# Causal attention and a PReLU MLP on one core: sums of x ahead of ACT's rounding, one w_out decode later, w_in pieces three slots sooner

## Chip, core and metric

The kernel runs on one core of a Trainium2 chip. The metric is the device time of one execution in microseconds (us), as the median of several runs. The core's engines work beside each other, each through a queue of its own in program order: PE (TensorE: matrix products into PSUM), DVE (VectorE), ACT (ScalarE), POOL (GpSimd), and SP (SyncE), which here issues nearly all transfers between HBM and SBUF.

## What is computed

```python
def _attn_ref(q, k, v):
    scores = scale * np.matmul(q, k.transpose(0, 1, 3, 2))
    scores = np.where(mask, -1000000000.0, scores)
    scores = scores - np.max(scores, axis=-1, keepdims=True)
    attn = np.exp(scores)
    attn = attn / (np.sum(attn, axis=-1, keepdims=True) + 1e-09)
    return np.matmul(attn, v).astype(np.float32)

def _moe_ref(x, w_in, w_out, alpha):
    h = x @ w_in
    g = np.maximum(h, 0.0) + alpha * np.minimum(h, 0.0)
    return (g @ w_out).astype(np.float32)
```

There are 4 batches of 12 heads, 448 positions, 64 dimensions a head. The attention's output, laid out as 1792 tokens of 768 features, is x; w_in is 768 by 2048, w_out 2048 by 768. Both weights arrive as 64-bit floats and are turned into 32-bit ones on the core.

## The kernel before

**Two stages.** The attention handles 24 pairs of heads; the MLP follows and takes about two thirds of the time. The MLP's products are done in a rounded 32-bit format, so each operand is split in a high part (rounded by ACT, a copy with a change of type) and a low part (the operand minus its high part, on DVE or POOL), and three products stand for one. The first product also saves multiplications by working with sums and differences of blocks of x and w_in: T1 to T4 are sums over x, S1 to S4 over w_in.

**The attention's order** is written out by hand in the string `ORDER`. `attention` (a loop over rounds n) goes through its words; `XF+4` means "step XF for pair n - 4". A step issues its instructions on its engine at that place of the program, so the string fixes the order within each queue. In one round PE does the product with v (AV), the 448-wide scores (S2), the transposes (PT1, PT0, PT2, PT3) and the scores of the next pair (S0, S1). DVE does the row maxima (MX), the two transpose copies C00 and C21 and the reciprocal (RC). ACT does the exponentials (EX) and the other transpose copies (C10, C20, C30). POOL normalises (NO). For x, when AV of a pair is done, four steps read its result from one PSUM bank: XH rounds it on ACT (blocks "B"), XN rounds it on DVE (blocks "N"), XF forms the sums on DVE (one or two operations per pair, line 545, and for some pairs a copy), XL takes the low part on DVE (line 553), after which the bank is free. PSUM has eight banks, handed out in turn.

**Weights between the attention's steps.** A piece of weights is loaded by SP into one of two raw buffers (`load_next`), then: `abs` on ACT (line 243), `clamp` on POOL (246), four operations "D" on DVE (249, 253, 256, 257), the last of which frees the raw buffer, and `add` on POOL (260). A finished piece is rounded by `cast` on ACT and its low part taken by `sub` on POOL (291 for w_in, 320 for w_out). The tables `EARLY` and `FRONT` give, for each round, what of this is done: i0 to i3 are the four w_in pieces of a group g, o0 to o3 those of w_out. In them A is abs, C clamp, D:i:k are k operations of piece i, + is add, LD a load, T the high and low part of one of the sums T on POOL. `FRONT` is done at the round's start (step E2), `EARLY` at step ED, between the low part and the copies C00 and C21; casts and abs of rounds before 24 at the step EA, behind the last transposes and C30.

**Behind the attention.** Round 26 also holds products of the first MLP group (`h_plain`, hooks behind AV and C30) and the PReLU of h (`h_act`, lines 721 and 722, on DVE). Then a table `FIRST` gives slots 0 to 30. In each of slots 1 to 10 PE does one `h_plain`, in each of slots 11 to 30 one `o_half` (a 128 by 384 part of the second product, line 769, put into SBUF by ACT at line 775). Around it the slot's tasks are issued: first act, gh and gl (PReLU; high part of g on ACT, line 731; low part on POOL, line 735), then D, then the rest in the order of `KINDS`. `.1` stands for pieces of the second group (g = 1). th and tl are high and low part of a T (ACT line 394, DVE line 569), st stores them, S forms a sum of w_in on DVE (265). Slot 23's `o_half` is the first that needs g_X of the second column block (gh.1X, gl.1X). After slot 30 the groups g = 1 to 7 follow in a fixed cycle.

Of the kernel before, what the change touches and what calls it, by code (L numbers as in the profile page):

```python
# [24 lines left out]
EARLY = {  # L25
# [5 lines left out]
}  # L31
FRONT = {25: "D:4:4", 26: "+:5 A:6 A:7"}
LOADV = {0: 2, 1: 2, 2: 2, 3: 1, 9: 4, 10: 3, 12: 1, 13: 2, 14: 2, 15: 2}
TURNS = [(0, 0), (0, 1), (0, 2), (0, 5), (1, 0), (1, 1), (1, 3), (1, 4), (0, 3), (0, 4), (1, 2), (1, 5)]
ORDER = """
E2+4 LK+0 LQ+0 LT+4 NO00+3p NO10+3p MX11+2 NO21+3p NO11+3p EX10+2 EX11+2 MX20+2 NO20+3p MX21+2 EX20+2 NO30+3p MX00+2 EX00+2 AV+4 S2+2 LV+4 PT1+3 PT0+3 PT2+3 XH+4 EX21+2 MX01+2 EX01+2 C10+3a XN+4 MX30+2 XF+4 XL+4 EX30+2 ED+4 C00+3d C21+3d RC+2 NO01+2p C20+3a PT3+3 S0+1 S1+1 SF+1 C30+3a EA+4 MX10+1 ST+4
"""
FIRST = """
0: gh.0Y gh.0X gl.0Y gl.0X cast.o0.0 cast.o1.0
1: act.0Z gh.0W gl.0W sub.o0.0 sub.o1.0 cast.o2.0 cast.o3.0  # L40
2: gh.0Z gl.0Z sub.o2.0 abs.i0.1 th
3: sub.o3.0 clamp.i0.1 tl th
4: D.i0.1.2 abs.i1.1 tl
5: act.1Y act.1X D.i0.1.2 load clamp.i1.1
6: gh.1Y D.i1.1.2 add.i0.1
7: gl.1Y D.i1.1.2 load th
8: add.i1.1 tl th
9: tl
10: S.S1.1 th abs.i2.1
11: act.1W act.1Z clamp.i2.1 cast.S1.1  # L50
12: D.i2.1.2 sub.S1.1 tl
13: D.i2.1.2 load th cast.L1.1
14: add.i2.1 abs.i3.1 tl th sub.L1.1
15: clamp.i3.1 S.S2.1 tl cast.A22.1
16: D.i3.1.2 cast.A11.1 sub.A22.1 st
17: gh.1X D.i3.1.2 load cast.S2.1 sub.A11.1 S.S3.1
18: gl.1X add.i3.1 cast.S3.1 sub.S2.1
19: gh.1W S.S4.1 sub.S3.1 abs.o0.1
20: gl.1W cast.A12.1 clamp.o0.1
21: D.o0.1.1 sub.A12.1  # L60
22: D.o0.1.1
23: gh.1Z D.o0.1.2 load
24: gl.1Z add.o0.1
25: abs.o1.1
26: clamp.o1.1
27: D.o1.1.2
28: D.o1.1.2 load
29: add.o1.1
"""
SECOND = """  # L70
1: cast.o0.0 abs.o2.0 clamp.o2.0
# [46 lines left out]
def kernel(  # L118
# [15 lines left out]
    B, NPAIR, D, _, S = qt.shape  # L134
# [4 lines left out]
    LQ = S - NQ * QP  # L139
# [200 lines left out]
    T, vs, p3, masks, qd = {}, [], [], [], []  # L340
# [42 lines left out]
    def load_v_some(n):  # L383
        for _ in range(n):
            next(v_loads, 0)

    def load_v_next(p):


        load_v_some(LOADV.get(p, 0))  # L390

# [169 lines left out]
    def t_hi(eng):  # L561
        h, nm, k = t_now[0] = next(t_queue)
        copy(hi_of(h, nm, k), x_f32(h, nm, k), eng)

    def t_lo(eng):
        h, nm, k = t_now[0]
        x = x_f32(h, nm, k)
        l = x.bitcast(F32R)
        eng.tensor_tensor(out=l, in0=x, in1=hi_of(h, nm, k), op=ALU.subtract)
        store(late, h, nm, k, l)  # L570
# [10 lines left out]
    plan, front, behind_it = {}, {}, {}  # L581
# [230 lines left out]
    def ops(nm, g, n):  # L812
        run(going[nm, g][1], n)
# [50 lines left out]
    def plan_early():  # L864

        def name_of(i):
            return f"i{i}" if i < 4 else f"o{i - 4}"

        for table, to in ((EARLY, plan), (FRONT, front)):
            for n, todo in table.items():  # L870
                for w in todo.split():
                    kind, *arg = w.split(":")
                    rear = to is plan and kind in ("A", "cast") and n < len(pairs)
                    fns = (behind_it if rear else to).setdefault(n, [])
                    if kind == "D":
                        fns.append(lambda i=int(arg[0]), n=int(arg[1]): ops(name_of(i), 0, n))
                    elif kind == "LD":
                        fns.append(load_next)
                    elif kind == "T":
                        fns.append(lambda: (t_hi(nc.gpsimd), t_lo(nc.gpsimd)))  # L880
                    elif kind in ("cast", "sub"):
                        fns.append(lambda f={"cast": cast, "sub": sub}[kind], nm=arg[0]: f(nm, 0))
                    else:
                        f = {"A": abs_of, "C": clamp, "+": add}[kind]
                        fns.append(lambda f=f, i=int(arg[0]): f(name_of(i), 0))
# [17 lines left out]
    with tc.manual_schedule():  # L903
# [32 lines left out]
        open_v()  # L936
        last = len(pairs) - 1
        plan_early()

        v_loads = (x for b in range(B) for x in load_v(b))  # L940
# [136 lines left out]
```

## Time and profile before

| | us |
|---|---|
| median of 3 runs (lowest to highest) | 634.29 (633.94 to 634.79) |
| the profiled execution's own time | 633.13 |
| its span, first to last instruction | 631.4 |
| busy: PE / DVE / POOL / ACT | 613.5 / 505.0 / 396.5 / 275.9 |

The profile is taken from one execution. Its span is the time from the first to the last instruction; 1.7 us of that execution lie outside. Times in rows are counted from the span's start. A row of a timeline gives start, duration, engine, line, operation, output and input, number of instructions merged, and in brackets the idle time before it and what ended it. The ends of matmuls are modelled, so PE's busy time says little; where its next instruction starts says more.

### The profile page before, as it was taken

The page shows a single profiled execution, that of the slowest core. Times are in us where ns is not written, and L with a number is a line of the kernel's source. Part 1 is how long each engine was busy: PE and PEld are TensorE (multiplying, and loading weights), DVE is VectorE, ACT ScalarE, POOL GpSimd, SP SyncE. Part 2 cuts the span into 40 slices and gives each one's busy share as a digit, 9 for nine tenths or more (in the row PEclk, how much of TensorE's full clock was granted, in tenths as well). Part 3 has the DMA queues.
Part 4 walks back from the last instruction along what each step waited for, and adds up shares of the span by engine and source line. Part 5 has one row for each costly group of instructions (what it writes and reads, how often), then busy time and mean ns, then how long its engine had stood idle before and what let it go on. Part 6 is the DMA issues. An engine that isn't in the chain of part 4 may idle for free.

```text
span 631.4 us, 10823 instructions
## 1 busy us (share of the span) xinstructions
PE 613.5 (97%) x3528; PEld 534.9 (85%) x3528; DVE 505.0 (80%) x1117; ACT 275.9 (44%) x766; POOL 396.5 (63%) x530
## 2 busy tenths in 40 slices
PE   7899999999998899999999999999999999999996
PEld 4567676666877899999999999999999999999996
DVE  5598999999877779898789779878977997795363
ACT  5788797888342655232323323231333323232110
POOL 3455576857875767975676677667657766762120
PEclk9899999999999799999999999999999999999999
DMA  4873387732866557757756775675667667554535
GB/s 131 197 200 110 104 227 216 211 118 72 264 210 218 168 189 256 240 167 224 242 171 195 220 222 176 217 229 167 211 209 221 196 195 238 170 175 137 172 142 199
DMA packets 87736, 120.38 MB, mean 191 GB/s; under 512 B 12033, under 2 KB 64257, under 8 KB 87681
## 3 DMA queue, kind: packets, MB, share of 16 engines
q1 hardware_dynamic: 87520, 119.48, 61.6%
q8 instruction: 28, 0.46, 0.3%
q10 hardware_dynamic: 160, 0.23, 0.1%
q14 instruction: 28, 0.22, 0.1%
HBM read 105.00 MB, written 14.68 MB: 190 GB/s over the span
## 4 chain that ended last, share of the span: by engine, by line
PE 83%; DVE 6%; DMA 3%; POOL 2%; issue 2%; SPq 1%; ACT 1%; POOLq 0%; ACTq 0%; DVEq 0%
PE o L769 34%; PE heldY L676 11%; PE heldX L676 8%; PE a L491 6%; PE heldZ L676 5%; PE pt L472 5%; PE s L417 4%; PE s L409 3%; PE h_V L676 3%; PE heldW L676 2%; DMA v<-in_v_dram 2%; DMA low_N<-low_N 1%; DMA raw_i<-in_moe_w_in_dram 1%; DVE s L429 1%; POOL wo L320 1%
## 5 line engine op out<-in xcount | busy, mean ns | idle before, releaser
L777 DVE TENSOR_TENSOR acc<-o,acc 128x384 f32<-128x384 f32 x196 | 107.4, 551 | 69.6 <-PE o L769 69.2
L398 POOL TENSOR_SCALAR p<-p,rs 128x128 f32<-128x128 f32 (+3 forms) x164 | 80.0, 509 | 60.0 <-DVE rs L453 37.8
L444 ACT ACTIVATE p<-s,nm 128x256 f32<-128x256 f32 (+3 forms) x168 | 82.5, 498 | 23.1 <-DVE nm L429 22.0
L429 DVE CUSTOM_DVE_ANT_0 s<-s,mask 128x256 f32<-128x256 f32 (+3 forms) x168 | 70.8, 481 | 18.7 <-PE s L409 13.7
L769 PE MATMUL o<-wo,g_X 128*128 128x384 f32 x336 | 77.5, 338 | 2.1 <-POOL g_X L735 2.1
L769 PE MATMUL o<-wo,g_Z 128*128 128x384 f32 x336 | 77.4, 338 | 1.9 <-ACT acc L775 1.9
L769 PE MATMUL o<-wo,g_W 128*128 128x384 f32 x336 | 77.4, 338 | 0.3 <-POOL g_W L735 0.3
L769 PE MATMUL o<-wo,g_Y 128*128 128x384 f32 x336 | 77.3, 338 | 0.0
L769 PEld LDWEIGHTS o<-wo,g_X 128*128 128x128 f32 x336 | 61.0, 190 | 5.6 <-POOL g_X L735 2.4
L769 PEld LDWEIGHTS o<-wo,g_Z 128*128 128x128 f32 x336 | 60.9, 190 | 5.3 <-ACT acc L775 2.2
L769 PEld LDWEIGHTS o<-wo,g_W 128*128 128x128 f32 x336 | 60.8, 190 | 0.6 <-POOL g_W L735 0.6
L769 PEld LDWEIGHTS o<-wo,g_Y 128*128 128x128 f32 x336 | 60.8, 190 | 0.0
L491 PEld LDWEIGHTS a<-ptf,v 128*64 128x64 f32 x384 | 28.5, 136 | 34.1 <-issue 9.8
L472 PEld LDWEIGHTS pt<-ident,p 128*128 128x128 f32 x384 | 44.1, 143 | 14.3 <-issue 10.2
L260 POOL TENSOR_TENSOR y_i<-y_i,x_i 128x384 f32<-128x384 f32 x32 | 33.6, 1051 | 31.4 <-DVE x_i L257 31.4
L491 PE MATMUL a<-ptf,v 128*64 128x64 f32 (+3 forms) x384 | 49.6, 387 | 3.3 <-DMA v<-in_v_dram 1.9
L472 PE MATMUL pt<-ident,p 128*128 128x128 f32 x384 | 48.2, 277 | 2.7 <-ACT p L444 1.4
L394 ACT ACTIVATE ptf<-pt 128x512 f32<-128x512 f32 (+1 forms) x72 | 38.6, 581 | 8.3 <-PE pt L472 8.3
L260 POOL TENSOR_TENSOR y_o<-y_o,x_o 128x384 f32<-128x384 f32 x32 | 32.5, 1016 | 14.4 <-DVE x_o L257 14.4
L417 PE MATMUL s<-kr,qr 64*128 64x128 f32 (+2 forms) x288 | 40.5, 398 | 0.0
L243 ACT ACTIVATE x_i<-raw_i 128x384 f32<-128x384 f32 x32 | 17.8, 556 | 50.7 <-DMA raw_i<-in_moe_w_in_dram 50.7
L735 POOL TENSOR_TENSOR g_Z<-t_Z,g_Z 128x384 fp32r<-128x384 f32 (+1 forms) x16 | 20.3, 1268 | 31.1 <-ACT g_Z L731 31.1
(177 smaller groups left out, 1346.8 us busy)
## 6 DMA issues: line engine op xcount, KB each, us to landing
lo_T<-low_T SPq DMA_DIRECT2D x28, 512.0 KB, 4.7
lo_B<-low_B SPq DMA_DIRECT2D x25, 512.0 KB, 4.9
raw_i<-in_moe_w_in_dram SPq DMA_DIRECT2D x32, 384.0 KB, 3.8
raw_o<-in_moe_w_out_dram SPq DMA_DIRECT2D x32, 384.0 KB, 3.2
lo_T<-low_T SPq DMA_DIRECT2D x28, 384.0 KB, 3.9
lo_B<-low_B SPq DMA_DIRECT2D x25, 384.0 KB, 4.0
lo_N<-low_N SPq DMA_DIRECT2D x16, 512.0 KB, 4.9
lo_N<-low_N SPq DMA_DIRECT2D x16, 384.0 KB, 4.6
```

Source lines behind the costliest of these rows:

```text
L260: nc.gpsimd.tensor_tensor(out=y, in0=y, in1=xf, op=ALU.add)
L394: eng.activation(out, x, AF.Copy, scale=side)
L398: eng.tensor_scalar(out=out, in0=x, scalar1=side, scalar2=1.0, op0=ALU.mult, op1=ALU.mult)
L417: nc.tensor.matmul(ps[:, o : o + lim], T["q", p][half(j), i * QP : (i + 1) * QP], T["k", p][half(j), :lim], start=(o == 0), stop=(n > 0 or ...
L429: nc.vector.tensor_tensor_reduce(out=t, in0=t, in1=masks[1] if i == NQ else masks[0][:, (NQ - 1 - i) * QP :], scale=-SCALE, scalar=MOST_F3 ...
L444: nc.scalar.activation(T["p", p, i][:, j, : t.shape[1]], t, AF.Exp, scale=-1.0, bias=T.pop(("nm", p, i, j)), accum_out=T["sm", p][:, z : z ...
L472: nc.tensor.transpose(ps[:, j - js[0], c], t[:, j, c * QP : (c + 1) * QP], T["ident"])
L491: nc.tensor.matmul(out[half(j), c * QP :], vs[b % 2][:, hp, c, j], x[:, c * QP : S], start=(c == 0), stop=(c == NQ),)
L676: nc.tensor.matmul(ps, w[:, u, k * P : (k + 1) * P], x, start=(first and i == 0), stop=(i == len(mms) - 1), skip_group_check=True,)
L735: nc.gpsimd.tensor_tensor(out=l, in0=hts.pop((q, nm)), in1=h, op=ALU.subtract)
L769: nc.tensor.matmul(ps[:, :NH], x, w, start=(i == 0), stop=(i == 3 * GC - 1))
L777: nc.vector.tensor_tensor(out=a[:, cols], in0=ps[:, :NH], in1=a[:, cols], op=ALU.add)
```

## The change

In `ORDER` the step XF moves from behind MX30 to the place behind EX01, ahead of XN; XH, before the first of the second half's steps, moves behind both. In the rounds 20 to 26 of `EARLY` the casts, low parts, abs and clamps are spread over earlier rounds. A new table `REAR` takes three entries of round 26, the decode, load and addition of o3, to step EA. In `FIRST` the pieces of g = 1 come two to four slots sooner, i0's abs and clamp in slot 0, and gl.1X shares slot 17 with gh.1X.

```diff
-    22: "+:3 sub:L1 cast:A11", 23: "sub:A11 cast:A12 A:4", 24: "sub:A12 C:4 cast:L0 A:5",
-    25: "C:5 sub:L0 LD +:4 T D:5:4 LD", 26: "C:6 C:7 D:6:4 LD D:7:4 LD T T +:6 T +:7 T",
+    20: "+:3 cast:A11", 21: "sub:L1 cast:A12", 22: "sub:A11 cast:L0 A:4", 23: "sub:A12 C:4 A:5", 24: "sub:L0 C:5",
+    25: "LD +:4 T D:5:4 LD", 26: "C:6 C:7 D:6:4 LD T T +:6 T T",
 }
 FRONT = {25: "D:4:4", 26: "+:5 A:6 A:7"}
+REAR = {26: "D:7:4 LD +:7"}
...
-... PT2+3 XH+4 EX21+2 MX01+2 EX01+2 C10+3a XN+4 MX30+2 XF+4 XL+4 EX30+2 ED+4 C00+3d C21+3d ...
+... PT2+3 EX21+2 MX01+2 EX01+2 XF+4 XN+4 XH+4 C10+3a MX30+2 XL+4 EX30+2 ED+4 C00+3d C21+3d ...
...
 FIRST = """
-0: gh.0Y gh.0X gl.0Y gl.0X cast.o0.0 cast.o1.0
-1: act.0Z gh.0W gl.0W sub.o0.0 sub.o1.0 cast.o2.0 cast.o3.0
-2: gh.0Z gl.0Z sub.o2.0 abs.i0.1 th
-3: sub.o3.0 clamp.i0.1 tl th
-4: D.i0.1.2 abs.i1.1 tl
-5: act.1Y act.1X D.i0.1.2 load clamp.i1.1
-6: gh.1Y D.i1.1.2 add.i0.1
-7: gl.1Y D.i1.1.2 load th
-8: add.i1.1 tl th
-9: tl
-10: S.S1.1 th abs.i2.1
-11: act.1W act.1Z clamp.i2.1 cast.S1.1
-12: D.i2.1.2 sub.S1.1 tl
-13: D.i2.1.2 load th cast.L1.1
-14: add.i2.1 abs.i3.1 tl th sub.L1.1
-15: clamp.i3.1 S.S2.1 tl cast.A22.1
-16: D.i3.1.2 cast.A11.1 sub.A22.1 st
-17: gh.1X D.i3.1.2 load cast.S2.1 sub.A11.1 S.S3.1
-18: gl.1X add.i3.1 cast.S3.1 sub.S2.1
-19: gh.1W S.S4.1 sub.S3.1 abs.o0.1
-20: gl.1W cast.A12.1 clamp.o0.1
-21: D.o0.1.1 sub.A12.1
-22: D.o0.1.1
-23: gh.1Z D.o0.1.2 load
-24: gl.1Z add.o0.1
...
+0: gh.0Y gh.0X gl.0Y gl.0X abs.i0.1 clamp.i0.1 cast.o0.0 cast.o1.0
+1: act.0Z gh.0W gl.0W D.i0.1.2 sub.o0.0 sub.o1.0 cast.o2.0 cast.o3.0
+2: gh.0Z gl.0Z D.i0.1.2 load abs.i1.1 clamp.i1.1 sub.o2.0 th
+3: D.i1.1.2 add.i0.1 sub.o3.0 tl th
+4: D.i1.1.2 load tl
+5: act.1Y act.1X add.i1.1 th
+6: gh.1Y tl abs.i2.1
+7: gl.1Y clamp.i2.1 S.S1.1 th
+8: D.i2.1.2 tl cast.S1.1
+9: D.i2.1.2 load sub.S1.1 abs.i3.1 cast.L1.1
+10: add.i2.1 clamp.i3.1 sub.L1.1 th
+11: act.1W act.1Z tl
+12: D.i3.1.2 S.S2.1 cast.A22.1
+13: D.i3.1.2 load sub.A22.1 th
+14: add.i3.1 S.S3.1 cast.A11.1 tl
+15: cast.S2.1 sub.A11.1 th
+16: cast.S3.1 sub.S2.1 S.S4.1 tl
+17: gh.1X gl.1X sub.S3.1 abs.o0.1 st
+18: gh.1W gl.1W cast.A12.1 clamp.o0.1
+19: D.o0.1.1 sub.A12.1
+20: D.o0.1.1
+21: D.o0.1.2 load
+22: add.o0.1
+23: gh.1Z gl.1Z abs.o1.1
...
-        for table, to in ((EARLY, plan), (FRONT, front)):
+        for table, to in ((EARLY, plan), (FRONT, front), (REAR, behind_it)):
```

## Rows read from the trace of the kernel before

**Rows 1.** What PE waited for, whole span: total us, times, longest.
```profile
PE o L769 <- POOL g_X L735: 2.1, 1, 2.1
...
PE o L769 <- ACT acc L775: 1.9, 1, 1.9
...
PE h_Y L676 <- DVE ptf L396: 0.7, 1, 0.7
```
**Rows 2.** The chain that ended last: start, us, what.
```profile
37.91 1.50 PE s L417 x12
...
50.06 1.73 PE s L417 x12
...
133.68 1.94 PE s L417 x11
...
146.27 1.94 PE s L417 x11
...
215.08 9.82 PE o L769 x46
...
299.45 2.08 PE o L769 x12
```
**Rows 3.** Timeline of ACT, rounds 21 and 25.
```profile
133.53 0.66 ACT L444 ACTIVATE p<-s,nm 128x448 f32<-128x448 f32 x1
...
158.40 0.53 ACT L394 ACTIVATE xw<-a 128x448 fp32r<-128x448 f32 x1
158.82 0.58 ACT L444 ACTIVATE p<-s,nm 128x384 f32<-128x384 f32 x1
```
**Rows 4.** Timeline of DVE, rounds 21 and 25.
```profile
131.97 0.63 DVE L429 CUSTOM_DVE_ANT_0 s<-s,mask 128x448 f32<-128x448 f32 x1 [0.38 <-PE s L409]
...
133.59 0.61 DVE L553 TENSOR_TENSOR low_B<-a,wi_x 128x448 fp32r<-128x448 f32 x1
...
158.97 0.62 DVE L545 TENSOR_TENSOR acc<-a,acc 128x448 f32<-128x448 f32 x1
```
**Rows 5.** The page's costliest groups: busy, mean ns, idle before and its releaser.
```profile
L398 POOL TENSOR_SCALAR p<-p,rs 128x128 f32<-128x128 f32 (+3 forms) x164 | 80.0, 509 | 60.0 <-DVE rs L453 37.8
L444 ACT ACTIVATE p<-s,nm 128x256 f32<-128x256 f32 (+3 forms) x168 | 82.5, 498 | 23.1 <-DVE nm L429 22.0
```
**Rows 6.** Timeline of PE, rounds 25 and 27.
```profile
159.64 0.63 PE L472 MATMUL pt<-ident,p 128*128 128x128 f32 x4 [0.54 <-ACT p L444]
...
182.48 1.20 PE L676 MATMUL h_Y<-xw,wi_A 128*128 128x512 f32 x4
```
**Rows 7.** What DVE waited for, 182.5 to 216 us.
```profile
DVE x_i L249 <- POOL x_i L246: 4.3, 2, 3.4
DVE xp L396 <- PE a L491: 2.3, 1, 2.3
DVE acc L569 <- ACT xw L394: 1.6, 1, 1.6
```
**Rows 8.** Timeline of DVE, 177 to 213 us.
```profile
177.18 0.88 DVE L396 COPY ptf<-pt 128x256 f32<-128x256 f32 x2
...
208.62 1.98 DVE L569 TENSOR_TENSOR acc<-acc,xw 128x448 fp32r<-128x448 f32 x2
...
212.02 0.89 DVE L249 TENSOR_SCALAR x_i<-x_i 128x384 int32<-128x384 int32 x1 [0.83 <-POOL x_i L246]
```
**Rows 9.** Groups of POOL, 182.5 to 216 us: busy us, mean ns, idle before.
```profile
L260 POOL TENSOR_TENSOR y_i<-y_i,x_i 128x384 f32<-128x384 f32 x4 | 4.8, 1191 | 10.1 <-DVE x_i L257 10.1
...
L735 POOL TENSOR_TENSOR g_X<-t_X,g_X 128x512 fp32r<-128x512 f32 x1 | 1.6, 1572 | 0.0
L291 POOL TENSOR_TENSOR wi_A<-y_i,wi_A 128x256 fp32r<-128x256 f32 x2 | 1.5, 786 | 0.0
```
**Rows 10.** Windows: stretch, length, busy of PE, PEld, DVE, ACT, POOL (instructions).
```profile
212.02:215.84 3.82, 1.71 (x10) 1.39 (x9) 3.71 (x5) 0.12 (x1) 3.01 (x3) 1.00 0.33 123
225.41:227.41 2.00, 2.00 (x13) 1.97 (x12) 1.84 (x4) 0.67 (x3) 0.00 (x0) 1.00 0.36 140
```

More of the change, by code (lines that the diff above doesn't have):

```diff
@@ L35 @@
 ORDER = """
-E2+4 LK+0 LQ+0 LT+4 NO00+3p NO10+3p MX11+2 NO21+3p NO11+3p EX10+2 EX11+2 MX20+2 NO20+3p MX21+2 EX20+2 NO30+3p MX00+2 EX00+2 AV+4 S2+2 LV+4 PT1+3 PT0+3 PT2+3 XH+4 EX21+2 MX01+2 EX01+2 C10+3a XN+4 MX30+2 XF+4 XL+4 EX30+2 ED+4 C00+3d C21+3d RC+2 NO01+2p C20+3a PT3+3 S0+1 S1+1 SF+1 C30+3a EA+4 MX10+1 ST+4
+E2+4 LK+0 LQ+0 LT+4 NO00+3p NO10+3p MX11+2 NO21+3p NO11+3p EX10+2 EX11+2 MX20+2 NO20+3p MX21+2 EX20+2 NO30+3p MX00+2 EX00+2 AV+4 S2+2 LV+4 PT1+3 PT0+3 PT2+3 EX21+2 MX01+2 EX01+2 XF+4 XN+4 XH+4 C10+3a MX30+2 XL+4 EX30+2 ED+4 C00+3d C21+3d RC+2 NO01+2p C20+3a PT3+3 S0+1 S1+1 SF+1 C30+3a EA+4 MX10+1 ST+4
@@ L54 @@
-15: clamp.i3.1 S.S2.1 tl cast.A22.1
-16: D.i3.1.2 cast.A11.1 sub.A22.1 st
-17: gh.1X D.i3.1.2 load cast.S2.1 sub.A11.1 S.S3.1
-18: gl.1X add.i3.1 cast.S3.1 sub.S2.1
-19: gh.1W S.S4.1 sub.S3.1 abs.o0.1
-20: gl.1W cast.A12.1 clamp.o0.1
-21: D.o0.1.1 sub.A12.1
-22: D.o0.1.1
-23: gh.1Z D.o0.1.2 load
-24: gl.1Z add.o0.1
[L64 to L68, printed above, removed]
+0: gh.0Y gh.0X gl.0Y gl.0X abs.i0.1 clamp.i0.1 cast.o0.0 cast.o1.0
+1: act.0Z gh.0W gl.0W D.i0.1.2 sub.o0.0 sub.o1.0 cast.o2.0 cast.o3.0
@@ L69 @@
+18: gh.1W gl.1W cast.A12.1 clamp.o0.1
[4 more added lines that the diff above has]
+23: gh.1Z gl.1Z abs.o1.1
+24: clamp.o1.1
+25: D.o1.1.1
+26: D.o1.1.1
+27: D.o1.1.2 load
+28: add.o1.1
 """
```

## The prediction

> **What bounds the kernel now.** I read the page first, then the waits of PE, then the chain of waits, then the queues of DVE, ACT and POOL where PE had stood. PE ends almost every stretch, so a change is worth what it takes out of PE's idle time, and the waits of PE name the places: 2.1 us for g_X from POOL, 1.9 us for an eviction by ACT, 0.7 us for a bank that a transpose copy of DVE holds [rows 1]. All three lie between the last attention rounds and the first MLP products. A second kind of loss does not show as a wait. In the chain the twelve score matmuls of a round take 1.50 us, but 1.73 to 1.94 us in some rounds [rows 2]; I count six such rounds, those whose pair carries two sums of x and that hold no decode of weights. In such a round ACT's last exponential starts at 133.53 [rows 3], and the scores of the next pair want that bank. That exponential is late because the whole loop through DVE is late: DVE stood 0.38 us for the 448-wide score product, worked from 131.97 to 133.59 on the maximum and the two sums, and only then took the low part, the transpose copies and the next maxima [rows 4]. Behind that stretch the waits of PE name nothing of this size; I take the rest as fixed work.
>
> **Part 1, sums in front (XF before XN, XH, and before MX30).** DVE now does the sums while PE still runs the 448-wide score product, for which it stood idle anyway. The gain per round is the smaller of that idle time (0.38 us in round 21) and the sum (0.62 us for one [rows 4], about twice that for two). PE loses some 0.3 us in each of the six rounds [rows 2], and cannot win more than that: 6 x 0.3 = 1.8, taken as **1.7 us**. In the rounds that hold decode work, DVE's own queue is the limit; there the low part must also wait for the rounding, which now stands behind two exponentials on ACT, so what DVE saves it waits for again. I take 0 there, between -0.6 and +0.8 for all of them. Behind the rounding on ACT stand the copy C10, the last exponential and C20; the same instructions as before, so they start when they did, unless the rounding has to wait for the sums.
>
> ACT's rounding and DVE's sums read the same bank, and they do not overlap: in round 25 the rounding runs 158.40 to 158.93 [rows 3] and the sum starts at 158.97 [rows 4], 0.04 us behind it. So with the sums in front the rounding waits for them. The Trainium skill, PSUM — Partial Sum Buffer, section "PSUM bank collisions raise a hardware error", asks for just this: two engines' accesses of one bank are to be guarded, reads against reads too. By it the rounding, and the low part after it, would come as late as before in rounds with two sums, and the 1.7 would shrink towards 0; the trace agrees that the two don't overlap. I put the new wait at nothing: the two exponentials that now precede it, the wider of 0.58 us [rows 3], fill ACT for most of the time that the sums take.
>
> Round 25 gains something else. Its transposes stand until 159.64 for an exponential [rows 6]; that exponential (158.82) was queued behind the rounding (158.40) [rows 3]. With the rounding behind it, it starts 0.42 us sooner: **0.4 us**; the bounds are 0 and 0.5.
>
> **Part 2, casts and low parts of w_in for g = 0 spread over rounds 20 to 24, abs and clamp of w_out one round sooner.** ACT's cast of 0.5 us goes behind C30, where ACT waits for DVE's maxima (22.0 us in all over the rounds), and POOL's additions go behind the normalising, where POOL waits for the reciprocal (37.8 us in all, 1.6 a round) [rows 5]; a round gets at most one addition (1.2) or two low parts (0.8 each) [rows 9]. Taken as 0; if the cover is gone, one round would lose up to 0.5 us.
>
> **Part 3, the last w_out piece (o3) decoded behind the last transposes.** In round 26 DVE's two decodes end at 177.2 and only then come the two transpose copies [rows 8], for which PE's next product waited 0.7 us [rows 1]. Now one decode stands ahead and the copies come as the transposes end: **0.7 us**. The second decode follows the PReLU of Y and X, and has the time until the last attention product ends at 182.48 [rows 6], before which DVE had 2.3 us with nothing to do [rows 7]; alone it needs 1.84 us, beside POOL up to 3.7 us [rows 10]. In the second case it delays the last low part by up to 1 us. The raw buffer of o3 comes free later, so SP issues i1.1's load after the low-part load that waits for PE. Its data are wanted only 6 us behind that, so this is 0; the bound is 1 us.
>
> **Part 4, pieces of w_in three slots sooner.** Count from t0, the end of the last attention product (182.48). PE's wait ends with g_X at 215.08 [rows 2], t0 + 32.6. Whether PE waits earlier for ACT (the 1.9 us) decides nothing: PE would only stand longer at g_X. So the price is the time at which POOL ends g_X.
> Before, DVE starts the fourth piece (i3) at 212.02 [rows 8], t0 + 29.5, having waited 4.3 + 1.6 us on the way for clamps and for ACT [rows 7]. Those waits come from ACT's abs behind late loads; with the loads sooner they go. New queue: 29.5 - 5.9 = 23.6; two low parts of T (1.98 us for both [rows 8]) now come behind this point, 21.6; one wait is left, for the clamp of the second piece, which stands on POOL behind three subtractions for w_out and two for g: about 1.5, 23.1. The first piece now runs beside POOL's work: four operations that take 1.84 us alone took 3.71 us (five operations) with POOL busy [rows 10], 1.8 more: **24.9**. Its bounds are 21.6 (no wait, no collision) and 29.7 (the slower rival). On SP the raw loads now stand in slots 2 and 4, behind a load of low parts that waits for PE's product of that slot, done long before; the stores of T that queue behind them are read only by g = 1: 0.
> But g_X has moved too. In POOL's queue it stood behind the third piece's addition and two low parts; now it also stands behind the fourth piece's addition and the low part of S2. So: 24.9 + 2.0 for the fourth decode (POOL has nothing left but what waits for it, so I take the lonely row), + 1.2 addition + 0.8 + 0.8 low parts + 1.6 for g_X [rows 9] = t0 + 31.3, against 32.6: **1.3 us**. The 46 matmuls behind the wait took 9.82 us, at the later rate of 2.08 for twelve 7.97 [rows 2]; I leave these 1.85 us as they are.
>
> What speaks against the change is that sharing. The rows show it: the same work 3.71 us beside POOL and 1.84 us without [rows 10]. The Trainium skill, SBUF — State Buffer, section "Who interferes with whom", says that DVE's second port pair is GpSimd's only one, held for a whole instruction. By it each of the four operations may wait out a whole addition; the trace agrees in direction.
>
> **Sum.** 1.7 + 0.4 + 0.7 + 1.3 = 4.1 us. Span 631.4 - 4.1 = 627.3; with the 1.7 us around it 629.0, against 633.1 of the profiled execution. That one lies 1.2 us under the median of 634.29, so the forecast is **630.2 us**.
>
> **Rivals.** *Slower: g_X ends later.* On POOL, g_X now hangs on the whole fourth piece. If the second and the fourth decode collide with POOL as well (2 x 1.8) and DVE waits 1.5 us at each of the last two clamps, it ends at 31.3 + 3.6 + 3.0 = t0 + 37.9, 5.3 us late; less the 2.8 us of the other parts, 2.5 us slower: 636.8. It decides once g_X is more than 4.1 us later than before. For it: the 3.71 us, and a queue one piece longer; against: POOL's share falls once w_out's low parts are done. The sharing rule above is this rival's mechanism.
> *No change.* The rounding, behind two exponentials and the sums, makes the low part as late as before (1.7 and 0.4 gone), and g_X gains nothing: 0.7 us, 633.6. For it: the low part needs the rounding; against: ACT's free time before each round's first exponential [rows 5]. The bank rule above is this rival's mechanism.
> *More.* The first decode meets no collision and no clamp wait is left: g_X at 31.3 - 1.8 - 1.5 = t0 + 28.0, 4.6 instead of 1.3: 7.4 us, 626.9. For it: the 1.84 us; against: the eight instructions that POOL has in slots 1 to 3.
>
> **Numbers.** A measurement of this kernel can tell about 0.2%, 1.3 us, from no change. Forecast, 1.3 to 5.9 us faster: 0.60. More than that: 0.12. Within 1.3 us: 0.16. Slower: 0.12. So faster 0.72. The range goes from the far rival, 626.9, to 635.0, which takes in the no-change rival and leaves out most of the slower one and the tail beyond the far one.
>
> **What would show it.** Right: no stretched score steps of 1.7 to 1.9 us; sums right behind MX01; no wait of PE for a transpose copy near 177; ACT no longer stopped by a load; one long wait of PE for g_X, ending some 4 us earlier than 215. Wrong: g_X released later than t0 + 32.6, or PE idle for weights at the first step of g = 1.

## The result, and the profile after

The changed kernel takes **629.7 us** as the median of 4 runs (627.45 to 629.98), the kernel before 634.54 (4 runs, 633.94 to 635.7): ratio 0.9914, 95% interval 0.9887 to 0.9941. That is 4.8 us faster, against 4.1 forecast (629.7 against 630.2). The profiled execution of the changed kernel is its quickest, 627.45 us with a span of 625.7; the one of before had 633.13 and 631.4. So the two profiles differ by 5.7 us, and about 1 us of that is the choice of execution.

First the waits of PE over the whole span, of the changed kernel (total us, times, longest):

```profile
PE a L491 <- DMA v<-in_v_dram: 2.3, 3, 1.2
PE o L769 <- ACT g_X L731: 1.8, 1, 1.8
...
PE o L769 <- POOL g_X L735: 1.1, 1, 1.1
...
PE o L769 <- ACT acc L775: 0.5, 1, 0.5
```

Of the three waits of before [rows 1], the one for the transpose copy is gone, the one for the eviction fell from 1.9 to 0.5 us, and the one for g_X is now two waits in a row, 1.8 for its high part and 1.1 for its low part. The chain of waits (start, us, what):

```profile
50.31 1.50 PE s L417 x12
...
119.43 4.61 DMA v<-in_v_dram
...
133.19 1.50 PE s L417 x12
...
145.34 1.50 PE s L417 x12
...
211.24 8.25 PE o L769 x46
```

The stretched score steps of 1.73 and 1.94 us [rows 2] are all 1.50 now. A load of v stands in the chain, as one did before (4.11 us at 120.42); PE now waits 0.77 us for it, and waited 0.22 before. And the 46 matmuls behind the wait for g_X took 8.25 us where they had taken 9.82.

With t0 for the end of the last attention product, and "held product" for the first product of the next group (tile heldY, g = 1), the 5.7 us divide like this (rounds are counted from one transpose step to the next):

| stretch | before | after | gained |
|---|---|---|---|
| start to t0 | 182.48 | 179.59 | 2.9 |
| t0 to the end of the wait for g_X | 32.60 | 31.65 | 0.95 |
| from there to the first product held for g = 1 | 9.66 | 8.09 | 1.6 |
| the rest of the span | 406.66 | 406.37 | 0.3 |

In round 21 the sums now stand where DVE had been idle. DVE's timeline, then ACT's, of the changed kernel:

```profile
130.54 0.62 DVE L545 TENSOR_TENSOR acc<-a,acc 128x448 f32<-128x448 f32 x1
131.08 0.61 DVE L396 COPY acc<-a 128x448 f32<-128x448 f32 x1
131.61 0.62 DVE L429 CUSTOM_DVE_ANT_0 s<-s,mask 128x448 f32<-128x448 f32 x1
...
132.37 0.62 DVE L553 TENSOR_TENSOR low_B<-a,wi_x 128x448 fp32r<-128x448 f32 x1
```
```profile
131.79 0.55 ACT L394 ACTIVATE wi_x<-a 128x448 fp32r<-128x448 f32 x1 [0.23 <-DVE acc L396]
...
132.71 0.64 ACT L444 ACTIVATE p<-s,nm 128x448 f32<-128x448 f32 x1
```

Before, the maximum came first (131.97), then the sums, and the low part at 133.59 [rows 4]; now the low part follows the maximum directly. The rounding waits 0.23 us until the sums, which read the same bank, are done; the last exponential comes all the same 0.82 us sooner (132.71 against 133.53 [rows 3]). Of this the round brought 0.5 us along, as its transposes start at 131.28 and started at 131.77; the other 0.3 are its own.

Round 26 and t0, on PE and then on DVE:

```profile
170.85 2.06 PE L472 MATMUL pt<-ident,p 128*128 128x128 f32 x16
...
174.86 1.08 PE L676 MATMUL h_Y<-xw,wi_A 128*128 128x512 f32 x4
...
179.59 1.20 PE L676 MATMUL h_Y<-xw,wi_A 128*128 128x512 f32 x4
```
```profile
171.71 0.42 DVE L396 COPY ptf<-pt 128x256 f32<-128x256 f32 x1 [1.60 <-PE pt L472]
...
175.07 0.76 DVE L249 TENSOR_SCALAR x_o<-x_o 128x384 int32<-128x384 int32 x1
```

DVE now waits 1.60 us for the transposes instead of making them wait, and decodes o3 at 175.07, behind the PReLU. From the transposes to t0 it is 8.74 us, where it was 9.70.

Last, the way to g_X: DVE (the first decode of g = 1, then the fourth), POOL, ACT and PE.

```profile
183.15 0.84 DVE L249 TENSOR_SCALAR x_i<-x_i 128x384 int32<-128x384 int32 x1
184.03 1.25 DVE L253 SCALAR_TENSOR_TENSOR y_i<-raw_i,x_i 128x384 int32<-128x384 int32 x1
185.32 1.06 DVE L256 TENSOR_SCALAR x_i<-y_i 128x384 int32<-128x384 int32 x1
186.41 1.25 DVE L257 SCALAR_TENSOR_TENSOR x_i<-raw_i,x_i 128x384 f32<-128x384 uint32 x1
189.05 1.16 DVE L249 TENSOR_SCALAR x_i<-x_i 128x384 int32<-128x384 int32 x1 [1.38 <-POOL x_i L246]
...
204.30 0.35 DVE L249 TENSOR_SCALAR x_i<-x_i 128x384 int32<-128x384 int32 x1
```
```profile
206.52 1.32 POOL L260 TENSOR_TENSOR y_i<-y_i,x_i 128x384 f32<-128x384 f32 x1 [2.62 <-DVE x_i L257]
207.81 0.91 POOL L291 TENSOR_TENSOR wi_A<-y_i,wi_A 128x256 fp32r<-128x256 f32 x1
208.67 1.11 POOL L291 TENSOR_TENSOR wi_S<-S,wi_S 128x256 fp32r<-128x256 f32 x1
209.75 1.44 POOL L735 TENSOR_TENSOR g_X<-t_X,g_X 128x512 fp32r<-128x512 f32 x1
```
```profile
205.60 0.42 ACT L287 ACTIVATE wi_S<-S 128x256 fp32r<-128x256 f32 x1 [2.72 <-DVE S L265]
...
208.16 0.42 ACT L287 ACTIVATE wi_S<-y_i 128x256 fp32r<-128x256 f32 x1 [1.29 <-DVE y_i L265]
...
208.85 0.62 ACT L731 ACTIVATE g_X<-t_X 128x512 fp32r<-128x512 f32 x1
```
```profile
209.53 0.61 PE L769 MATMUL o<-wo,g_X 128*128 128x384 f32 x2 [1.79 <-ACT g_X L731]
211.24 0.45 PE L769 MATMUL o<-wo,g_X 128*128 128x384 f32 x1 [1.11 <-POOL g_X L735]
...
219.33 0.39 PE L667 MATMUL heldY<-xw,wi_A 128*128 128x512 f32 x1
```

The four operations beside POOL took 4.40 us (1.84 alone [rows 10]); the one clamp wait is 1.38; the fourth piece starts at 204.30, t0 + 24.7. Neither engine lacks g_X's input: on ACT two casts of S ahead of it wait for DVE (2.72 and 1.29 us), on POOL the addition and two low parts stand ahead of it.

### The profile page after: what moved, and what is told of

It reads as the page before. It is cut to its first block, busy times and chain, and to the rows that moved or that the text cites. A ratio compares the mean times of both kernels' runs of the same rounds, so it can differ in the third digit from the quotient of the medians.

```text
span 625.7 us, 10851 instructions
## 1 busy us (share of the span) xinstructions
PE 608.4 (97%) x3528; PEld 529.6 (85%) x3528; DVE 501.7 (80%) x1117; ACT 277.2 (44%) x766; POOL 395.7 (63%) x530
## 4 chain that ended last, share of the span: by engine, by line
PE 82%; DVE 6%; DMA 4%; SPq 3%; POOL 2%; ACT 1%; issue 1%; POOLq 0%; ACTq 0%; DVEq 0%
PE o L769 35%; PE heldY L676 11%; PE heldX L676 8%; PE heldZ L676 5%; PE pt L472 5%; PE a L491 4%; PE s L417 3%; PE h_V L676 3%; PE heldW L676 2%; DMA v<-in_v_dram 2%; PE s L409 2%; SPq L352 2%; ACT p L444 1%; SPq L355 1%; DVE s L429 1%
## 5 line engine op out<-in xcount | busy, mean ns | idle before, releaser
L491 PEld LDWEIGHTS a<-ptf,v 128*64 128x64 f32 x384 | 27.7, 136 | 35.1 <-issue 10.5
L417 PE MATMUL s<-kr,qr 64*128 64x128 f32 (+2 forms) x288 | 38.4, 394 | 0.0
```

Of the source, the lines that this page charges most:

```text
L417: nc.tensor.matmul(ps[:, o : o + lim], T["q", p][half(j), i * QP : (i + 1) * QP], T["k", p][half(j), :lim], start=(o == 0), stop=(n > 0 or ...
L491: nc.tensor.matmul(out[half(j), c * QP :], vs[b % 2][:, hp, c, j], x[:, c * QP : S], start=(c == 0), stop=(c == NQ),)
```

## Experiments: the parts one by one

The diff ahead of the prediction has the words in full; here stands which part each kernel takes. All ratios are to the kernel before, run beside the kernel in question.

**The new order alone.**

```diff
-... PT2+3 XH+4 EX21+2 MX01+2 EX01+2 C10+3a XN+4 MX30+2 XF+4 XL+4 ...
+... PT2+3 EX21+2 MX01+2 EX01+2 XF+4 XN+4 XH+4 C10+3a MX30+2 XL+4 ...
```

> The kernel before with the new ORDER alone (sums ahead of the rounding). Theory, sums fill DVE's idle time: the stretched score steps of rounds 8 to 11, 21 and 23 go back to 1.50 us and the transposes of round 25 wait some 0.4 us less, so the last attention product ends 1.4 to 2.1 us sooner; everything behind it keeps its distance (g_X 32.6 us behind that end): 632.8 us, 1.7 us faster. Rival, the loads of v set the rounds: the gain is given back while PE waits for v in rounds 8 and 20, under 0.6 us faster in all. Rival, the gain in rounds 20 to 25 came from the thinner EARLY rounds: about 0.9 us faster, from rounds 8 to 11 alone.

Measured: 633.27 against 634.66 us, 0.9975 (0.9961 to 0.9988): 1.4 us (1.6 by the ratio). The score steps lost their stretch. In the profile t0 comes only 0.85 us sooner, not the 1.4 to 2.1 expected: round 8 starts 1.35 us later than before, 0.82 of it for a wait for v at 48.38. Of round 25's gain almost nothing was left (0.07 us). Its transposes waited 0.33 us instead of 0.54, but the next attention product took 2.32 us instead of 2.08, as DVE's copies came late. They stood behind a low part that waited 0.55 us for the rounding, and behind a decode beside POOL with one operation of 1.40 us. DVE of this kernel in round 25, then PE behind the attention:

```profile
159.19 0.62 DVE L553 TENSOR_TENSOR low_B<-a,xw 128x448 fp32r<-128x448 f32 x1 [0.55 <-ACT xw L394]
...
160.46 1.40 DVE L253 SCALAR_TENSOR_TENSOR y_o<-raw_o,x_o 128x384 int32<-128x384 int32 x1
```
```profile
210.97 0.62 PE L769 MATMUL o<-wo,g_X 128*128 128x384 f32 x2 [0.90 <-ACT g_X L731]
214.51 0.69 PE L769 MATMUL o<-wo,g_X 128*128 128x384 f32 x1 [2.92 <-POOL g_X L735]
...
225.19 0.39 PE L667 MATMUL heldY<-xw,wi_A 128*128 128x512 f32 x1
```

What PE saves ahead of t0 it waits for at g_X in part: the wait is 2.92 us, and from its end to the held product it is 10.68 us, not 9.66.

**The w_out decode and the spread casts alone** (`EARLY`, `REAR`).

```diff
-    ... 25: "C:5 sub:L0 LD +:4 T D:5:4 LD", 26: "C:6 C:7 D:6:4 LD D:7:4 LD T T +:6 T +:7 T",
+    ... 25: "LD +:4 T D:5:4 LD", 26: "C:6 C:7 D:6:4 LD T T +:6 T T",
+REAR = {26: "D:7:4 LD +:7"}
```

> The kernel before with the new EARLY and REAR alone. Theory: only the transpose copies of round 26 come sooner, PE's wait of 0.7 us for them goes and the rest keeps its distance: 633.8 us, 0.7 us faster. Rival, the casts and abs taken out of rounds 22 to 24 also shorten rounds: 1.2 us faster, seen as earlier transposes in rounds 23 to 25. Rival, the later load of i1 and the later low part of the last pair cost as much as that: no change.

Measured: 634.56, ratio 1.0001 (0.9982 to 1.0021). In its profile the stretch from round 26's transposes to t0 is 8.74 us, the 0.96 gained, and the wait for the copy is gone. The median doesn't show it, and where it went is not shown: the profiled execution took 636.32 us, 1.8 above the median. In it two stretches took more than before: the wait for g_X (0.9 + 2.9) with 10.5 us behind it where there were 9.66, and a wait of 2.51 us for v at 48.07. That round lies ahead of everything this part touches, so the v wait is not its doing.

**The sooner pieces of w_in alone** (`FIRST`).

```diff
-2: gh.0Z gl.0Z sub.o2.0 abs.i0.1 th
...
-17: gh.1X D.i3.1.2 load cast.S2.1 sub.A11.1 S.S3.1
-18: gl.1X add.i3.1 cast.S3.1 sub.S2.1
...
+0: gh.0Y gh.0X gl.0Y gl.0X abs.i0.1 clamp.i0.1 cast.o0.0 cast.o1.0
...
+17: gh.1X gl.1X sub.S3.1 abs.o0.1 st
```

> The kernel before with the new FIRST alone. Theory, g_X hangs on the fourth piece's decode and the low parts ahead of it on POOL: the last attention product ends as before, g_X comes 31.3 to 31.9 us behind it instead of 32.6, PE's wait for ACT's eviction falls from 1.9 to under 1 us without that mattering: 1.0 us faster, 633.5 us; with the slow stretch of PE behind g_X gone as well, up to 2.6 us. Rival, PE's arrival and not g_X decides: 2 us or more faster by the shorter wait for ACT alone, with PE reaching the product after g_X is there. Rival, no decode of o3 moved: the decode of the last w_out piece is in the way of the first slots and g_X comes no sooner: no change.

Measured: 633.96, ratio 0.9991 (0.9969 to 1.0013), no difference that can be told. The wait ends at t0 + 31.64, the same 0.96 us sooner as in the whole change; but behind it 10.8 us pass in this execution instead of 9.66, and that gives it back there. As that stretch differs from one execution to the next (see the last section), the median neither shows the 0.96 us nor rules them out.

**The whole change again.** The kernel is unchanged, so there is no diff; a second profile was to show whether the 8.09 us behind the wait belong to the change.

> The changed kernel once more, for more runs and a second profile. Theory, the stretch behind g_X ran at the full clock only by chance in the first profile (8.1 us from g_X to the first product of the next group, against 9.7 before and 10.5 to 10.8 in the runs that changed one part): this profile shows a slow stretch there, 10 us or more, and a median near 630 us. Rival, the changed kernel lacks the slow stretch as a rule: 8.1 us again and a median of 628 us or less.

Measured: 630.29 against 634.43 us, 0.9928 (0.9901 to 0.9955). The same two waits (1.8 and 1.1), the same t0 + 31.63, and then 9.51 us. So the 1.6 us of that stretch are not the change's; they vary from one execution to the next (see the last section).

**The whole change without the new order.**

```diff
-... PT2+3 EX21+2 MX01+2 EX01+2 XF+4 XN+4 XH+4 C10+3a MX30+2 XL+4 ...
+... PT2+3 XH+4 EX21+2 MX01+2 EX01+2 C10+3a XN+4 MX30+2 XF+4 XL+4 ...
```

> The changed kernel with the ORDER of the kernel before: new EARLY, REAR and FIRST. Theory, the parts add up: it lacks the 0.9 us of rounds 8 to 11, the 0.9 us of rounds 20 to 24 and the 0.4 us of round 25, so it is 1.7 to 2.2 us slower than the changed kernel, 631.7 us, with stretched score steps of 1.7 to 1.9 us back in rounds 8 to 11, 21 and 23. Rival, the three parts only pay together (1.6, 0 and 0.6 us alone against some 5 together): 4 us slower than the changed kernel.

Measured: 632.2, ratio 0.9966 (0.9948 to 0.9983), 1.9 us above the whole change measured beside it. So the order is worth about as much within the whole as alone (1.4 to 1.6), and the other parts together about 2.2.

**The sums in front, but the rounding ahead of the exponentials as before.** Only XH moves back.

```diff
-... PT2+3 EX21+2 MX01+2 EX01+2 XF+4 XN+4 XH+4 C10+3a ...
+... PT2+3 XH+4 EX21+2 MX01+2 EX01+2 XF+4 XN+4 C10+3a ...
```

> The changed kernel with only the rounding XH back at its old place ahead of EX21, the sums still ahead of MX30. Theory, DVE's sums and ACT's rounding share a bank and run one behind the other: the sums now wait for the rounding, DVE stands idle behind MX01 instead of in front of MX30, and in round 25 the exponentials wait for the rounding again; 0.5 to 1.2 us slower than the changed kernel, with score steps over 1.60 us in some of rounds 8 to 11 and 21 to 23. Rival, only the place of the sums counts and the rounding's place is free: as the changed kernel within 0.3 us, sums starting right behind MX01.

Measured: 633.34, ratio 0.9983 (0.9965 to 1.0002): 0.9 us below before where the whole change has 4.1 (0.9928, 0.9901 to 0.9955) and the whole without the new order 2.2. Its rounds 21 to 23 take 6.39 to 6.57 us, those of the whole change 6.08. DVE, ACT and PE of that kernel in round 21:

```profile
133.25 0.62 DVE L545 TENSOR_TENSOR acc<-a,acc 128x448 f32<-128x448 f32 x1 [0.71 <-ACT wi_x L394]
```
```profile
132.69 0.53 ACT L394 ACTIVATE wi_x<-a 128x448 fp32r<-128x448 f32 x1
...
135.10 0.63 ACT L444 ACTIVATE p<-s,nm 128x448 f32<-128x448 f32 x1 [0.48 <-DVE nm L429]
```
```profile
134.93 1.86 PE L417 MATMUL s<-kr,qr 64*128 64x256 f32 x12
```

With the rounding first, the sums wait 0.71 us for it, the maximum stands behind the sums, the last exponential waits for that maximum, and the score step is stretched again. So the gain is not in the sums' place alone: it needs the rounding behind them. Moving the sums alone is no better than moving nothing in `ORDER`; whether it is worse, by 1.3 us, the two intervals leave open. The fourth combination, the rounding behind the exponentials and the sums at their old place, was not tried, so what the rounding's move would give alone is not known. I had priced that move at nothing but round 25's 0.4.

## Experiments: what is left in g_X and in v

**g_X ahead of what waits for DVE.** On both queues g_X's parts go ahead of the fourth piece's addition and the casts and low parts of S2 and S3.

```diff
-14: add.i3.1 S.S3.1 cast.A11.1 tl
-15: cast.S2.1 sub.A11.1 th
-16: cast.S3.1 sub.S2.1 S.S4.1 tl
-17: gh.1X gl.1X sub.S3.1 abs.o0.1 st
-18: gh.1W gl.1W cast.A12.1 clamp.o0.1
+14: S.S3.1 cast.A11.1 tl
+15: sub.A11.1 th
+16: tl
+17: gh.1X gl.1X add.i3.1 cast.S2.1 sub.S2.1 S.S4.1 abs.o0.1 st
+18: gh.1W gl.1W cast.S3.1 sub.S3.1 cast.A12.1 clamp.o0.1
```

> The changed kernel, but the addition of the fourth piece, cast and low part of S2, S3's cast and S4 moved behind gh.1X and gl.1X (slots 17 and 18). Theory, POOL's and ACT's queue order alone holds g_X: g_X ends 25 to 27 us behind the last attention product instead of 31.6, PE's waits of 1.8 and 1.1 us for it go, 3 us faster than the changed kernel: 626.7 us, 7.8 us below the kernel before. Rival, the evictions by ACT and the banks are the next limit: half of that, 628.2 us. Rival, S2's and S3's low parts are then late for g = 1 and PE waits there: as the changed kernel, 629.7 us.

Measured: **625.7**, ratio 0.9868 (0.9844 to 0.9891), 3 to 5 us below the changed kernel, when each is set against the kernel before. POOL has g_X done at 205.5, and PE's waits for it are gone; from t0 to the first held product it is 36.27 us where the changed kernel had 39.74 and 41.14 in its two profiles and before 42.26. This stretch is 36.27 or 36.28 us in all four kernels that hold this edit, and 39.73 to 43.56 in the nine profiles without it. POOL's row, PE's waits, and the granted clock (windows: stretch, length, busy PE, PEclk, DMA share, GB/s):

```profile
204.14 1.40 POOL L735 TENSOR_TENSOR g_X<-t_X,g_X 128x512 fp32r<-128x512 f32 x1
```
```profile
PE heldY L676 <- DMA lo_T<-low_T: 0.9, 1, 0.9
...
PE heldX L676 <- DMA lo_B<-low_B: 0.7, 1, 0.7
```
```profile
210.00:220.00 10.00, 10.00 (x59) 1.00 0.34 111
```

What is late next are low parts that g = 1 reads back: 0.9 and 0.7 us.

**Loads of v sooner.** `LOADV` says how many loads of v are issued in each round. The one of round 3 goes to round 0, the two of round 15 to round 12.

```diff
-LOADV = {0: 2, 1: 2, 2: 2, 3: 1, 9: 4, 10: 3, 12: 1, 13: 2, 14: 2, 15: 2}
+LOADV = {0: 3, 1: 2, 2: 2, 9: 4, 10: 3, 12: 3, 13: 2, 14: 2}
```

> The changed kernel with the last loads of v for the second and the fourth batch issued one round sooner. Theory, part of what the sums in front win is spent waiting for v in rounds 8 and 20 (1.2 us together in the profile of the changed kernel, 1.2 to 3.1 us in the others): 1 to 1.5 us faster than the changed kernel, 628.5 us, waits of PE for v under 0.5 us behind 30 us. Rival, the transfers share the DMA engines with q and k, and v comes as late as before or q and k become late: no change.

Measured: 627.2, ratio 0.9872 (0.9847 to 0.9897), 3.1 us below the changed kernel measured beside it. Behind 30 us PE waits for v no more, and t0 comes at 178.47. It gives more than the profile of the changed kernel would allow, probably because that one was mild: it waited 0.8 us for v behind 30 us, its second profile 2.15 at one place. PE's wait for v in round 8 was between 0.8 and 2.5 us in seven of the ten profiles with the old `LOADV`, and under 0.4 in the other three.

**Both, and o0 and o1 of w_out sooner.** Three kernels: the g_X edit with the abs, clamp and decode of o0 and o1 one to three slots sooner; the g_X edit with the v loads; all three.

```diff
...
-18: gh.1W gl.1W cast.A12.1 clamp.o0.1
-19: D.o0.1.1 sub.A12.1
-20: D.o0.1.1
-21: D.o0.1.2 load
...
+18: gh.1W gl.1W D.o0.1.1 cast.S3.1 sub.S3.1
+19: D.o0.1.1 cast.A12.1 sub.A12.1
+20: D.o0.1.2 load abs.o1.1
+21: add.o0.1 clamp.o1.1
...
```

> The kernel with g_X sooner, and besides abs, clamp and decode of the next w_out pieces one to three slots sooner, so that the raw loads in SP's queue stand less long ahead of the loads of low parts. Theory, the waits of PE of 0.9 and 0.7 us for low parts of T and B in the first steps of g = 1 come from SP's queue, which stood at the raw loads: they fall under 0.5 us together, 1 us faster than g_X sooner: 624.7 us. Rival, the transfers themselves are late, from their stores or from crowded DMA engines: no change, 625.7 us. Rival, the decode now stands in the way of S2 and S3: PE waits for weights, slower than 625.7 us.

> g_X sooner and v sooner together, on the changed kernel. Theory, the two waits lie in different stretches and add: 3.8 us (g_X) and 3.1 us (v) less 0.8 us that the loads of low parts take back, some 10 to 11 us below the kernel before, 623.5 us; no wait of PE for v behind 30 us and none for g_X. Rival, with the attention shorter the loads of low parts for g = 1 are what PE waits for, 2 us or more: 625 us.

> As before, with abs, clamp and decode of the next w_out pieces sooner too. Theory, SP's queue is free sooner and PE's waits for low parts of T and B at the first steps of g = 1 stay under 0.9 us (1.6 without it): 0.5 to 1 us faster than without, 623 us. Rival, no difference from it that can be told: the same median within 0.8 us.

Measured: 626.81 (0.9876, 0.9848 to 0.9905); **623.76** (0.9827, 0.9804 to 0.9849); 623.33 (0.9824, 0.9804 to 0.9844). The sooner pieces of w_out halve the waits for low parts (0.5 and 0.3 us); a gain in time, of which 1 us had been expected, can't be told. The g_X edit and the v loads add up as far as can be told: 10.5 us below before, about 6 below the changed kernel, where 3 to 5 and 3.1 were to be had alone. Of the kernels tried, this is the one to keep.

## Why the prediction was right, and where its terms were off

**Sums in front, 1.7.** Right. The six rounds named gained 1.9 us, 1.0 in rounds 8 to 11 together and 0.44 each in rounds 21 and 23; all six take 6.08 us now, the shortest that any round takes in these kernels. Of this 1.1 us arrived at t0. Loads of v, no term of the sum, took back 0.8: 0.25 ahead of round 8, and 0.55 in round 19, at whose end PE waited 0.77 us for v (124.08). Decode rounds, taken as 0 between -0.6 and 0.8, gave 0.3, nearly all from one round (6.82 to 6.41 us). The no-change rival (the rounding comes too late) did not decide in the six rounds: the rounding's wait for the sums is there, 0.23 us in round 21, and costs nothing. In rounds 12, 15, 16 and 25 the low part does wait 0.55 us for the rounding, and rounds 15 and 16 are as long as before (6.78 and 6.65 us, 6.76 and 6.63 before), as the prediction had it for rounds with decode work. Before, in round 25, it was the sums that stood behind the rounding [rows 3, 4]. The Trainium skill, PSUM — Partial Sum Buffer, section "PSUM bank collisions raise a hardware error", wants two engines' accesses of one bank guarded; the rows agree: in no round of any kernel here do ACT's and DVE's reads of that bank overlap, in either order. What I had not seen is that with the sums in front the same guard makes the rounding's move necessary: without it 3 of the 4 us are gone.

**Round 25, 0.4.** Its transposes come through 0.37 us sooner (2.60 us to the next product instead of 2.97). With the order alone the next product gave that back. In the changed kernel the low part waits for the rounding just as long, but the decode behind it runs without collision, from 159.11 to 161.09:

```profile
158.56 0.62 DVE L553 TENSOR_TENSOR low_B<-a,xw 128x448 fp32r<-128x448 f32 x1 [0.55 <-ACT xw L394]
```

So the gain is kept only together with the spread additions and low parts of part 2, which I had priced at 0. From these transposes to those of round 26 it is 15.17 us and was 15.73: 0.56 for both parts.

**o3 behind the transposes, 0.7.** Measured 0.96: from round 26's transposes to t0 it is 8.74 us in all ten profiles with this part, and 9.66 or 9.70 in the three without. The wait of 0.7 us [rows 1] went, and with it some 0.3 us around it. The decode at 175.07 met POOL in its first operation alone (0.76 us), and DVE still had 2.3 us idle ahead of t0.

**g_X, 1.3.** This is the mis-sized term: 0.95. The wait ends at t0 + 31.63 to 31.65 in all six profiles with the new `FIRST` and this order of g_X's queues, and at 32.60 to 32.88 in the three with the old one. The start of the fourth decode was forecast at t0 + 24.9 and came at t0 + 24.7, out of errors that nearly cancel. The first piece lost 2.56 us to the collision instead of 1.8, though 0.3 of this was in the row started from; against that, the clamp wait was 1.38 instead of 1.5, the second piece took 0.2 less than before, and a sum for S2 had moved from ahead of the decode into it, 0.4. From there it took 6.9 us and not 6.4: the two low parts took 0.91 and 1.11 us beside DVE, not 0.8 each, and that operation for S2 stood within the decode. The Trainium skill, SBUF — State Buffer, section "Who interferes with whom", speaks of this sharing; the rows agree, with 4.40 against 1.84 us. The slower rival needed it for the second and fourth piece as well. The second met it (189.05, 1.16 us for an operation of 0.35), but it had met it before the change too (operations of 1.25 and 1.33 us at 198.24 and 199.53); the fourth, at 204.30, met none. Of ACT's wait for late loads, which I said would go, 1.3 us of 5.8 stayed. I had also counted on one long wait; PE stands twice, first for ACT, where I had said that ACT's place decides nothing. For the changed kernel that holds, as POOL ends later; the sum was right there.

**The 1.85 us behind the wait, left unchanged.** In the profile shown they went (8.09 us), in the repeat they came back (9.51). On the median the forecast of no change is the better one, and 4.1 forecast stands against 4.8 and 4.1 in the two comparisons. That it is so near is in part luck: in the profile the terms gave 1.1, 0.3, 0.56, 0.96 and 0.95, 3.9 in all, where 1.7, 0, 0.4, 0.7 and 1.3 were forecast, and what v and g_X took away the decode rounds, round 25 and o3 nearly made up.

**What is open.** Alone, the three parts give 1.4, 0.1 and 0.7 us, 2.2 together, and the whole 4.1 to 4.8. Each has an uncertainty of 0.9 to 1.4 us, so that they don't add up is not shown; round 25's gain, 0.56 together and 0.07 and 0.17 alone, is the one joint gain that the rows name. Why loads of v come late in some executions and not in others was not tried.

## What to carry to other kernels

When several engines read one bank in turn, the order of all of them is one decision: moving one to fill an idle place worked here only when the engine that shares the bank moved behind it. A wait at the end of a long queue is first a question of what stands ahead in that queue: moving the decodes forward brought g_X 0.95 us, moving what wasn't ready from in front of it another 3 to 5. And gains ahead of a wait that depends on another queue are paid back there, so price the next wait with each of them.

## What was not expected of the hardware

The time behind a broken run of PE is not fixed. Windows of the granted clock (stretch, length, PE busy, PEclk, DMA share, GB/s), of the kernel before, then with the order alone, then of the changed kernel:

```profile
215.90:219.50 3.60, 3.60 (x13) 0.53 0.33 109
```

```profile
211.00:214.50 3.50, 0.59 (x2) 0.84 0.55 210
214.50:219.80 5.30, 5.29 (x17) 0.50 0.27 74
```
```profile
209.50:211.20 1.70, 0.61 (x2) 1.00 0.89 340
211.20:219.30 8.10, 8.06 (x46) 1.00 0.19 52
```

Before, behind a wait of 2.11 us, PE ran for 3.6 us at a granted clock of 0.53, near its 1.2 GHz level; this is most of the 1.85 us that the prediction left as they are and did not name. After waits of 0.90 and 2.92 us PE ran for 5.3 us at 0.50, and 2.6 us were lost against 8.09. After 1.8 and 1.1 us it kept 1.00 in one profile; in the repeat, with the same two waits, a mean of 0.83 was granted from 210 to 220 us and 1.4 us were lost. In all there are six profiles with these same two waits. Over the 5.3 us behind them the granted clock was 1.00 in the changed kernel and with the rounding first, 0.73 with v sooner, 0.71 in the repeat, 0.68 without the new order and 0.50 with `FIRST` alone. From the end of the wait to the first held product they took 8.09, 8.83 (0.58 of it a further wait for ACT), 9.38, 9.51, 9.65 and 10.80 us. So these waits, 2.9 us in all, cost from 0 to 2.7 us more behind them, and their length did not settle how much. With g_X's waits gone the clock stayed at 1.00 over that stretch.
